# The opening of the last stage: a rewritten chain from the summed expert weights, sums moved to GpSimd, and part of a bound taken from the decoding

## The chip, the cores and the metric

One Trainium2 chip; the program runs on one of its cores. A core has TensorE (matrix products, results in the eight PSUM banks), VectorE, ScalarE and GpSimd (element by element), and SyncE, which here issues the transfers. The engines run their own instruction queues in order and wait for one another by semaphores. The metric is the device time of one execution in microseconds; before the change it is 865.24 us, the median of three runs (864.58 to 865.53).

## The reference

Eight heads of block-causal attention, then a soft mixture of experts, then a squared-ReLU feed-forward layer:

```python
scores = scale * q @ k.T;  scores = where(block_mask, scores, -1e9)
x = softmax(scores) @ v                        # (8, 8, 576, 64) -> (4608, 512)
logits = x @ phi                               # (4608, 32): 8 experts, 4 slots each
d = softmax(logits, over tokens);  slot_input = d.T @ x
slot_out[e] = relu(slot_input[e] @ w1[e]) @ w2[e]
x = softmax(logits, over slots) @ slot_out     # (4608, 512)
h = relu(x @ w_in)                             # w_in (512, 2048)
out = (h * h) @ w_out                          # w_out (2048, 512)
```

All is in float32. The slots are so few (32) that `slot_out @ w_in` can be formed first, a matrix of 32 x 2048, called `psw` in the kernel (laid out as four groups of 32 rows by 512 columns). Then `h` is the combine weights (32 wide) times that matrix.

## The kernel before, in words

Three stages follow one another: attention with the routing logits, the experts (`experts`), and the last stage (`ffn`). The change lies where the second passes into the third.

**The end of the experts.** The last weights of `w2` arrive in pieces, and `acc1` takes the products of the second group of four experts in two halves of 256 columns. Each half is copied to SBUF by ScalarE into `os` (one buffer), transposed by TensorE and copied into `so` by VectorE (`finish`), and two `fold`s per half then multiply it with `w_in` (decoded earlier, `tin`) into `psw`, one PSUM bank.

**From psw to the hidden layer.** `psw` is split into two float32r parts, `wf[0]` (rounded) and `wf[1]` (the remainder), first 128 columns, then 384; the larger piece goes through SBUF (`cts["w"]`) and GpSimd makes its two parts (lines 1408 and 1409). `spread(c)` selects one group of 32 rows for all partitions with a selector matrix `sel` (two matmuls, line 1418) and ScalarE copies it to `ws` (line 1421). `first_hidden(c)` multiplies `ws` with the combine weights of the first 512 tokens (line 1441), `relu_square` makes Relu and Square of it on ScalarE (lines 1430, 1431), and `first_product(c, a)` multiplies with the decoded `w_out` (`tt`) into the four banks of `pos` (line 1626). There are eight chunks `c` of two halves `a`.

**Decoding.** `w_out` arrives in pairs of words per number. `decode_mag` makes float32 numbers of a chunk: an Abs on ScalarE (line 234, with priority in the planner) and four operations on VectorE (lines 235, 236, 239, 242). Behind each chunk ScalarE takes the sum of absolute values of the decoded numbers (line 1397); the eight sums give a bound for the size of `w_out` (`scale_max`, line 1463), from which the power of two `beta` follows that scales the weights into float16. Through a transposition by TensorE (`scale_turn`, lines 1470 and 1482) the maximum over partitions gives `alpha` and others.

**The first four token tiles and the blocks.** The first 512 tokens are computed in float32 as above. All later tokens go in blocks of 256 through a seven-product scheme: sums and differences of four quarters of the weights (`sum_w`, T3 to T6, 128 x 2048 each), casts to a float16 high part by ScalarE (`cast_w`, B0 to B6, line 1547) and a low part by VectorE (`low_w`, L0 to L6, line 1550); and for the activations of a block, in four parts `kq`, hidden matmuls (`block_first`, H, line 1568), Relu and Square (`block_square`, q), four sums or differences of 128 x 256 (`block_sums`, s, lines 1581 and 1536), casts (`block_cast`, c, line 1591) and low parts (`block_low`, l, line 1536). Seven products (line 1604) follow for each block.

**What sets the order.** TensorE's, VectorE's and ScalarE's instructions from chunk 4 on are in the order of the string `ORDER` (its letters are those above; `h`, `g` and `m` are hidden matmuls, Relu and Square, and product of a chunk; `n`, `z`, `b`, `a` are the scale's four steps). Ahead of it, where the stage opens, and always for GpSimd, a planner puts the instructions in order by its own costs and by the place where they stand in the program; instructions with priority go first. Inside a region with a written order, instructions from outside may still fall between. The hidden matmuls, the spreads, the transposed maximum and the block's hidden matmuls share two PSUM tiles of two banks each (`bank2`); `psw`'s bank goes to whichever pool is opened first after it.

Of the kernel before, what the change touches and what calls it, by code (L numbers as in the profile page):

```python
# [23 lines left out]
def tile_attn_soft_moe_ffn(  # L24
# [31 lines left out]
    ORDER = (  # L56
# [171 lines left out]

    def decode_mag(pool, dst, raw, w):
# [5 lines left out]
        nc.vector.tensor_scalar(out=m, in0=m, scalar1=2.0 ** -15, scalar2=None, op0=ALU.max)  # L235
        nc.vector.tensor_scalar(
            out=b, in0=b, scalar1=3, scalar2=0x3FFFFFF8, op0=ALU.logical_shift_left, op1=ALU.bitwise_and
        )
        nc.vector.scalar_tensor_tensor(
            out=b, in0=hi, scalar=0xC0000000, in1=b, op0=ALU.bitwise_and, op1=ALU.bitwise_or  # L240
        )
        nc.vector.scalar_tensor_tensor(
            out=dst.bitcast(U32), in0=lo, scalar=29, in1=b, op0=ALU.logical_shift_right, op1=ALU.bitwise_or
        )

# [905 lines left out]
    def experts():  # L1151
# [117 lines left out]
        for x in acc1:  # L1269
            nc.vector.memset(x, 0.0)  # L1270
        for c in range(8):
# [92 lines left out]
    def ffn():  # L1364
# [17 lines left out]
        sums = ws_p.tile([128, KH], F32, name="sums")  # L1382
        mg = ws_p.tile([128, 2], F32, name="mg")
        sc = {nm: ws_p.tile([128, 1], F32, name=nm) for nm in ("beta", "alpha", "inv", "sg", "se")}
        sc.update(zip(("top", "sw"), cts["tiny"][2:]))
        al = [sc["alpha"]] + cts["tiny"][:2]
        wf = [d_p.tile([128, 512], F32R, name=f"wf{i}", bufs=1) for i in range(2)]
        tt = t_p.tile([128, KH, 2, DM], F32, name="t")

        def decode_wo(c, a=None):  # L1390
            sl = slice(0, 2) if a is None else slice(a, a + 1)
            w = DM * (sl.stop - sl.start)
            raw = wos[c][:, sl].rearrange("p a f x -> p (a f) x")
            decode_mag(d_p, tt[:, c, sl].rearrange("p a f -> p (a f)"), raw, w)
            if a != 0:
                jk = d_p.tile([128, 2, DM], mybir.dt.bfloat16, tag="jk", name="jk", bufs=1)
                nc.scalar.activation(out=jk, in_=tt[:, c], func=AF.Abs, accum_out=sums[:, c:c + 1])

        psw = wots["psw"]
        parts = (slice(0, 128), slice(128, 512))  # L1400
        p = parts[0]
        nc.scalar.copy(wf[0][:, p], psw[:, p])
        nc.vector.tensor_tensor(out=wf[1][:, p], in0=psw[:, p], in1=wf[0][:, p], op=ALU.subtract)
        p = parts[1]
        wfs = cts["w"][:, p]
        nc.scalar.copy(wfs, psw[:, p])
        nc.scalar.copy(cts["w"][:, parts[0]], psw[:, parts[0]])
        nc.gpsimd.tensor_copy(wf[0][:, p], wfs)
        nc.gpsimd.tensor_tensor(out=wf[1][:, p], in0=wfs, in1=wf[0][:, p], op=ALU.subtract)
        decode_wo(0, 0)  # L1410
# [4 lines left out]
        def spread(c, p=slice(0, 512)):  # L1415
            ps = bank2("ps_ws")
            for i in range(2):
                nc.tensor.matmul(
                    ps[:, p], cts["sel"][:, c, 32 * i:32 * i + 128], wf[i][:, p], start=(i == 0), stop=(i == 1)
                )  # L1420
            nc.scalar.copy(ws[:, 512 * c + p.start:512 * c + p.stop], ps[:, p])

# [9 lines left out]

        def first_hidden(c, step=1024, late=False):
            ps = bank2("ps_h")
            if late:
                hid[c] = lambda: first_square(c, ps)
            else:
                g = g_p.tile([128, 1024], F32, tag="g", name="g")
            for a in range(2):
                f = c + KH * a  # L1440
                nc.tensor.matmul(
                    ps[:, 512 * a:512 * a + T0], ws[:, 128 * f:128 * f + 128], ctt[:, 0:T0], start=True, stop=True
                )
                if step == 512:
                    relu_square(ps, g[:, 512 * a:512 * a + 512], 512 * a, 512 * a + 512, scale=1.0 / CSC)
                    if a == 0:
                        spread(2, parts[0])
            if late:
                return
            if step == 1024:  # L1450
                relu_square(ps, g, 0, 1024, scale=1.0 / CSC)
            return g

# [81 lines left out]

        sub = lambda o, a, b: nc.vector.tensor_tensor(out=o, in0=a, in1=b, op=ALU.subtract)  # L1536
# [41 lines left out]
        def block_sums(n, kq):  # L1578
            x = a7[n, kq]
            z = lambda s: x[:, :, s]  # L1580
            nc.vector.tensor_tensor(out=z(4), in0=z(1), in1=z(3), op=ALU.add)
            sub(z(1), z(0), z(1))
            sub(z(5), z(4), z(0))
            sub(z(6), z(2), z(5))

# [13 lines left out]
        def product(n, sa, sb, acc, first):  # L1599
# [9 lines left out]
        pos = [ps_o.tile([128, DM], F32, tag="o", name="po") for _ in range(N0)]  # L1609
        spread(0, parts[0])  # L1610
        hid = {0: first_hidden(0, 512)}
        decode_wo(0, 1)
        spread(0, parts[1])
        spread(2, parts[1])
        nc.vector.tensor_reduce(
            out=mg[:, 0:1], in_=wf[0].bitcast(F32), axis=AX.X, op=ALU.max, apply_absolute_value=True
        )
        spread(1)
        spread(3)
        for c in range(1, KH):  # L1620
            decode_wo(c)

        def first_product(c, a):
            g = hid[c]
            for t in range(N0):
                nc.tensor.matmul(  # L1626
# [77 lines left out]

        for c in range(3):
            hid[c + 1] = first_hidden(c + 1)
            for a in range(2):
                first_product(c, a)
        E = mybir.EngineType
# [82 lines left out]
```

## Time and profile before

| | |
|---|---|
| median of three runs | 865.24 us |
| the profiled execution | 864.24 us |
| its span | 862.4 us |
| TensorE busy | 810.9 us (94%) |
| VectorE busy | 670.2 us (78%) |
| ScalarE busy | 626.9 us (73%) |
| GpSimd busy | 241.5 us (28%) |

The profile shows one execution. In its tables PE is TensorE and PEld its weight loads, DVE is VectorE, ACT is ScalarE, POOL is GpSimd. A row of a timeline gives the start, the duration, engine, line and operation, output and input tiles with shapes, and a count; in brackets the time for which the engine stood idle before it and what ended that. Matmuls are pipelined, so the duration of one in such a row holds its way through the array, and the rate is read from several in a row. PEclk is the granted clock of TensorE as a share of 2.4 GHz. The experts end at about 464 us of the span, the last stage runs from there to the end; the string `ORDER` begins at about 496 us and the first block product stands at 536.5 us.

### The profile page before, as it was taken

The numbers are of one execution on the slowest core, as the hardware profiler recorded it, in microseconds if no ns is written. First come the engines' busy times: TensorE is split into PE (matmuls) and PEld (weight loads), VectorE is DVE, ScalarE is ACT, GpSimd is POOL, SyncE is SP. The second block draws the span as 40 slices with busy tenths as digits, with TensorE's granted clock in tenths as the row PEclk, the third lists the DMA queues.
The fourth block names the chain that finished last, engine by engine and source line by source line (L and its number), as shares of the span: only waits on it lengthen the run. The fifth ranks groups of instructions, "written<-read, shape, count | busy, mean of one in ns | idle before, by whom it ended". The sixth has DMA issues, their size and how long they took to land.

```text
span 862.4 us, 21655 instructions
## 1 busy us (share of the span) xinstructions
PE 810.9 (94%) x8741; PEld 597.5 (69%) x8741; DVE 670.2 (78%) x1546; ACT 626.9 (73%) x996; POOL 241.5 (28%) x394
## 2 busy tenths in 40 slices
PE   2699999998999999999986999999999999999997
PEld 1366767575766667676432454888888888888886
DVE  5877789899899987764726899888888888888880
ACT  5588787787878687743225899988888888878770
POOL 0255747376574757464000000000000000000000
PEclk9899999999999999999998999999999999999999
DMA  7997998989898979589899100110000000000002
GB/s 156 194 192 132 186 216 151 223 160 224 156 215 163 197 124 197 90 251 373 335 401 397 57 0 25 39 37 25 26 25 27 25 26 25 26 25 26 26 25 49
DMA packets 213316, 113.14 MB, mean 131 GB/s; under 512 B 192096, under 2 KB 194144, under 8 KB 213216
## 3 DMA queue, kind: packets, MB, share of 16 engines
q1 hardware_dynamic: 210560, 111.11, 54.0%
q8 instruction: 68, 1.11, 0.5%
q10 hardware_dynamic: 2656, 0.66, 0.4%
q14 instruction: 32, 0.26, 0.1%
HBM read 78.71 MB, written 9.44 MB: 102 GB/s over the span
## 4 chain that ended last, share of the span: by engine, by line
PE 73%; DMA 8%; ACT 6%; POOL 6%; DVE 5%; issue 2%; SPq 0%; ACTq 0%; POOLq 0%
PE ps_y L1604 15%; PE ps_z L1604 10%; PE ps_x L1604 10%; PE xm L655 8%; PE ps_sc L581 6%; DMA t<-qb 4%; PE ps_hb L1568 3%; DMA wch<-in_moe_w_dram 3%; PE sm L675 3%; POOL ul L771 3%; PE ps_max L503 2%; POOL ss L624 2%; PE po L1626 2%; PE tl L666 2%; PE ps_qT L482 2%
## 5 line engine op out<-in xcount | busy, mean ns | idle before, releaser
L1604 PEld LDWEIGHTS <-ah 128*128 128x128 f16 x1792 | 174.8, 98 | 21.9 <-issue 0.8
L619 ACT ACTIVATE p<-ps_sc,es 128x512 f32<-128x512 f32 x192 | 129.7, 685 | 59.1 <-PE ps_sc L581 29.8
L1536 DVE TENSOR_TENSOR al<-a,ah 128x1024 f16<-128x1024 f32 (+1 forms) x128 | 138.5, 1124 | 16.9 <-ACT ah L1591 15.3
L517 DVE TENSOR_REDUCE pm<-ps_max 128x4 f32<-128x512 f32 x160 | 106.0, 681 | 32.6 <-PE ps_max L511 32.3
L624 POOL TENSOR_TENSOR ss<-p 128x384 f32<-128x384 f32 (+1 forms) x128 | 85.7, 688 | 152.4 <-ACT p L619 152.0
L1591 ACT CAST ah<-a 128x1024 f16<-128x1024 f32 (+1 forms) x128 | 114.4, 936 | 15.0 <-DVE a L1536 13.4
L581 PE MATMUL ps_sc<-t,s 128*128 128x512 f16 (+3 forms) x512 | 107.0, 302 | 11.7 <-DMA t<-qb 6.6
L1697 POOL TENSOR_TENSOR ot<-u,p 128x256 f32<-128x256 f32 x16 | 12.5, 781 | 373.6 <-DVE u L1668 357.9
L1604 PE MATMUL ps_y<-bh,al 128*128 128x256 f16 x384 | 104.7, 273 | 0.0
L1604 PE MATMUL ps_y<-bh,ah 128*128 128x256 f16 x384 | 104.6, 272 | 0.0
L1604 PE MATMUL ps_y<-bl,ah 128*128 128x256 f16 x384 | 104.6, 272 | 0.0
L624 POOL TENSOR_TENSOR ss<-ss,p 128x320 f32<-128x320 f32 (+1 forms) x128 | 97.9, 765 | 16.9 <-ACT p L619 9.1
L1604 PEld LDWEIGHTS <-al 128*128 128x128 f16 x896 | 87.6, 98 | 10.2
L1430 ACT ACTIVATE r<-ps_hb,cts_h 128x1024 f32<-128x1024 f32 x64 | 71.2, 1112 | 30.0 <-PE ps_hb L1568 29.4
L655 PE MATMUL xm<-p,ar_hi 128*64 128x256 f32 (+3 forms) x512 | 87.2, 440 | 0.0
L1536 DVE TENSOR_TENSOR a<-a 128x256 f32<-128x256 f32 x192 | 76.1, 424 | 3.9
L1604 PE MATMUL ps_x<-bh,ah 128*128 128x256 f16 x256 | 69.8, 273 | 0.0
L1604 PE MATMUL ps_z<-bh,ah 128*128 128x256 f16 x256 | 69.8, 273 | 0.0
L1604 PE MATMUL ps_x<-bh,al 128*128 128x256 f16 x256 | 69.8, 273 | 0.0
L1604 PE MATMUL ps_x<-bl,ah 128*128 128x256 f16 x256 | 69.8, 273 | 0.0
L1604 PE MATMUL ps_z<-bl,ah 128*128 128x256 f16 x256 | 69.8, 273 | 0.0
L1604 PE MATMUL ps_z<-bh,al 128*128 128x256 f16 x256 | 69.8, 273 | 0.0
(275 smaller groups left out, 1779.3 us busy)
## 6 DMA issues: line engine op xcount, KB each, us to landing
wch<-in_moe_w_dram SPq DMA_DIRECT2D x18, 1024.0 KB, 10.9
ar_hi<-in_v_dram SPq DMA_DIRECT2D x64, 128.0 KB, 3.8
raw<-in_moe_w_in_dram SPq DMA_DIRECT2D x16, 512.0 KB, 5.5
out_dram<-ot SPq DMA_DIRECT2D x32, 256.0 KB, 2.1
ar_hi<-in_moe_w_dram SPq DMA_DIRECT2D x6, 1024.0 KB, 7.8
s<-s SPq DMA_DIRECT2D x32, 144.0 KB, 4.1
ar_hi<-in_k_dram SPq DMA_DIRECT2D x16, 256.0 KB, 4.5
ar_hi<-in_q_dram SPq DMA_DIRECT2D x16, 256.0 KB, 4.2
```

The lines of the kernel that those rows point to most:

```text
L517: nc.vector.tensor_reduce(out=o, in_=i, axis=AX.X, op=ALU.max)
L581: nc.tensor.matmul(ps[:, c0:c0 + w].rearrange("p (s c) -> p s c", c=128), kk[:, 2 * t + hp, :], qq[:, 2 * u0 + hp:8:2, :], start=(c0 == 0 ...
L619: exps[:] = [nc.scalar.activation(out=pt, in_=ps, func=AF.Exp, scale=es[:, 0:1])]
L624: add = lambda o, x, y: nc.gpsimd.tensor_tensor(out=o, in0=x, in1=y, op=ALU.add)
L655: nc.tensor.matmul(box["xm"][64 * hp:64 * hp + 64, 128 * t:512], vs[:, t, hp, :], r, start=(t == 0), stop=(t == 3),)
L675: nc.tensor.matmul(SM[b][32 * g:32 * g + 32, o0:o0 + w], oj, r, start=bool(start and j == 0), stop=stop, tile_position=(0, 32 * g), skip_g ...
L771: add = lambda o, x, y: nc.gpsimd.tensor_tensor(out=o, in0=x, in1=y, op=ALU.add)
L1430: nc.scalar.activation(out=r[:, c0:c1], in_=ps[:, c0:c1], func=AF.Relu, **kw)
L1536: sub = lambda o, a, b: nc.vector.tensor_tensor(out=o, in0=a, in1=b, op=ALU.subtract)
L1568: nc.tensor.matmul(ps[:, 512 * j + 256 * a:512 * j + 256 * a + 256], w[:, 128 * f:128 * f + 128], c, start=True, stop=True,)
L1591: nc.scalar.copy(v(hl[n % 2][0][:, 2 * kq:2 * kq + 2], s), v(a7[n, kq], s))
L1604: nc.tensor.matmul(acc[:, 0:HM], a[:, k], b[:, k], start=bool(first and k + j == 0), stop=(k == KH - 1 and j == 2), skip_group_check=not f ...
```

## The change

In `experts`, the transposes of the first half are done ahead of the last piece of weights, and the folds of the first half are no longer both ahead of the second half's transposes. In the last stage, the opening is written out in order for three engines (`opening`): the two-part split of the larger piece of `psw` goes to ScalarE and VectorE, spreads are done for two groups at a time with one copy, filler matmuls of 256 columns (`spin`, 7 and 5 of them) are put ahead of the first spread and the first hidden matmuls, half of the first Relu and Square goes to VectorE, and the pools of PSUM are opened in the other order. The four operations of `decode_mag` become a list to be placed. For chunks 5 to 7 the first of them also folds its maximum into `tops`, and `scale_max` makes a bound of that (three more small operations); the absolute sums by ScalarE stay for chunks 0 to 4. `sum_w` 4, 5 and 6 and the block sums of the first block go to GpSimd, and `ORDER` is changed.

```diff
     ORDER = (
-        "O h4 n m30 b g4 T3 B2 T4 z m31 B0 a B4 L2 h5 B1 H00 m40 L0 g5 L4 q00 H01 m41 L1 q01 s00 h6 "
-        "B3 H02 s01 m50 c00 T6 c01 m51 l00 g6 l01 q02 h7 L3 g7 H03 m60 s02 q03 T5 m61 c02 s03 B6 "
-        "l02 m70 c03 L6 B5 m71 l03 L5 H10 o0 o1 X P1 ...
+        "O h4 n m30 b g4 T3 B2 T4 z m31 B0 a L2 h5 B1 H00 m40 L0 g5 L1 q00 H01 m41 B3 q01 s00 h6 "
+        "L3 T5 B4 H02 s01 m50 c00 c01 m51 l00 g6 l01 L4 T6 q02 h7 g7 H03 m60 s02 q03 m61 B5 c02 s03 "
+        "L5 l02 m70 c03 B6 m71 l03 L6 H10 o0 o1 X P1 ...
...
+        kw = {} if top is None else dict(op1=ALU.max, accum_out=top)
+            lambda: nc.vector.tensor_scalar(out=m, in0=m, scalar1=2.0 ** -15, scalar2=None, op0=ALU.max, **kw),
...
+                if c == 7 and kt == 7:
+                    tail.pop(0)()
...
-            pend.append(lambda dts=dts, os_=os_: [finish(1, dts, os_)] + [fold(dt) for dt in dts])
-        pend.pop()()
+            tail.append(lambda dts=dts, os_=os_: finish(1, dts, os_))
+        for f in (lambda: fold(0), tail.pop(0), lambda: fold(1), lambda: fold(2), lambda: fold(3)):
+            f()
...
+        d0, d1 = decode_wo(0, 0), decode_wo(0, 1)
+        for f in d0:
+            f()
         psw_st.close()
+        ps_o = st.enter_context(tc.tile_pool(name="ps_o", bufs=4, space=PSUM))
         ps_h = st.enter_context(tc.tile_pool(name="ps_h", bufs=2, space=PSUM))
-        ps_o = st.enter_context(tc.tile_pool(name="ps_o", bufs=4, space=PSUM))
...
         def scale_max():
+            x, y = tops.bitcast(U32), top_b.bitcast(U32)
+            ts(out=y, in0=x, scalar1=3, scalar2=0x3FFFFFF8, op0=ALU.logical_shift_left, op1=ALU.bitwise_and)
+            nc.vector.scalar_tensor_tensor(
+                out=y, in0=x, scalar=0xC0000000, in1=y, op0=ALU.bitwise_and, op1=ALU.bitwise_or
+            )
+            ts(out=sums[:, NABS:KH], in0=top_b, scalar1=4.5, scalar2=None, op0=ALU.mult)
             nc.vector.tensor_reduce(out=sg, in_=sums, axis=AX.X, op=ALU.add)
...
-            sub(x, a, b)
+            sub(x, a, b, nc.vector if s == 3 else nc.gpsimd)
...
+            e = nc.vector if n else nc.gpsimd
+            e.tensor_tensor(out=z(4), in0=z(1), in1=z(3), op=ALU.add)
+            sub(z(1), z(0), z(1), e)
+            sub(z(5), z(4), z(0), e)
+            sub(z(6), z(2), z(5), e)
...
+        def opening():
+            p0, p1 = slice(0, 128), slice(128, 512)
+            w = cts["w"]
+            nc.scalar.copy(wf[0][:, p0], psw[:, p0])
+            dec.tensor_tensor(out=wf[1][:, p0], in0=psw[:, p0], in1=wf[0][:, p0], op=ALU.subtract)
+            nc.scalar.copy(w, psw)
+            spin(pos[0], SPINS[0])
+            spread((0, 2), p0)
+            nc.scalar.copy(wf[0][:, p1], w[:, p1])
+            for f in d1[:3]:
+                f()
+            dec.tensor_tensor(out=wf[1][:, p1], in0=w[:, p1], in1=wf[0][:, p1], op=ALU.subtract)
+            spin(pos[0], SPINS[1])
...
+            pre = spread((0, 2), p1, False)
+            pre.pop(0)()
...
+            nc.scalar.activation(out=r[:, h0], in_=ps[:, h0], func=AF.Relu, scale=1.0 / CSC)
+            dec.tensor_scalar(
+                out=r[:, h1], in0=ps[:, h1], scalar1=1.0 / CSC, scalar2=0.0, op0=ALU.mult, op1=ALU.max
+            )
+            nc.scalar.activation(out=g[:, h0], in_=r[:, h0], func=AF.Square)
+            dec.tensor_tensor(out=g[:, h1], in0=r[:, h1], in1=r[:, h1], op=ALU.mult)
+            d1[3]()
+            first_product(0, 0, (0, 1))
+            pre.pop(0)()
+            first_product(0, 0, (2, 3))
+            ds = decode_wo(1)
...
+            pre.pop(0)()
+            first_product(0, 1, (0,))
+            first_hidden(1)
+            first_product(0, 1, (1, 2, 3))
+            for f in ds:
+                f()
+            dec.tensor_reduce(
+                out=mg[:, 0:1], in_=wf[0].bitcast(F32), axis=AX.X, op=ALU.max, apply_absolute_value=True
+            )
+            spread((1, 3))
+            size(0)
+
+        with tc.manual_schedule(engines={E.PE, E.DVE, E.Activation}):
+            opening()
```

## Rows read from the trace of the kernel before

**Rows 1.** Stages: start:end, length, busy (x count) per engine, PEclk, DMA, GB/s

```profile
464.30:470.14 5.84, 1.11 (x6) 0.79 (x6) 5.58 (x8) 5.25 (x11) 1.97 (x2) 0.84 1.03 409
...
496.74:521.73 24.99, 24.20 (x72) 12.08 (x71) 24.65 (x30) 24.32 (x21) 0.00 (x0) 1.00 0.00 0
...
536.50:558.00 21.50, 21.50 (x202) 18.21 (x201) 16.95 (x32) 19.94 (x24) 0.79 (x1) 1.00 0.10 38
```

**Rows 2.** The same view in slices of 0.2 us, where the clock changes

```profile
468.20:468.40 0.20, 0.00 (x0) 0.00 (x0) 0.20 (x1) 0.20 (x1) 0.00 (x0) 0.66 0.97 389
...
475.00:475.20 0.20, 0.20 (x1) 0.12 (x1) 0.20 (x1) 0.00 (x0) 0.00 (x0) 0.78 1.23 492
```

**Rows 3.** Timeline of TensorE, 458 to 522 us

```profile
458.46 0.61 PE L1279 MATMUL po<-wch,hT 128*4 128x256 f32 x8 [0.82 <-DMA wch<-in_moe_w_dram]
...
462.31 1.92 PE L1211 MATMUL psw<-tin,so 128*32 128x512 f32 x16 [0.29 <-DVE so L1204]
...
466.20 0.44 PE L1418 MATMUL ps_ws<-wf,sel 128*128 128x128 f32 x2 [1.97 <-ACT cts_h L1407]
...
470.14 2.08 PE L1626 MATMUL po<-t,g 128*128 128x512 f32 x2 [2.06 <-ACT g L1431]
...
481.43 1.02 PE L1441 MATMUL ps_h<-cts,ws 128*128 128x512 f32 x2
...
489.61 7.03 PE L1626 MATMUL po<-t,g 128*128 128x512 f32 x16
496.07 1.02 PE L1441 MATMUL ps_h<-cts,ws 128*128 128x512 f32 x2
...
521.73 0.74 PE L1568 MATMUL ps_hb<-cts,ws 128*128 128x256 f32 x4 [0.79 <-ACT r L1430]
```

**Rows 4.** Timeline of VectorE, 460 to 522 us

```profile
460.54 0.43 DVE L235 TENSOR_SCALAR dec_mag<-dec_mag 128x512 f32<-128x512 f32 x1 [0.87 <-ACT dec_mag L234]
...
467.15 0.67 DVE L1615 TENSOR_REDUCE mg<-wf 128x1 f32<-128x512 f32 x1
467.75 1.43 DVE L239 SCALAR_TENSOR_TENSOR dec_mag<-ar_hi,dec_mag 128x1024 uint32<-128x1024 uint32 x1
...
478.47 0.69 DVE L235 TENSOR_SCALAR dec_mag<-dec_mag 128x1024 f32<-128x1024 f32 x1 [1.84 <-ACT dec_mag L234]
...
488.54 1.23 DVE L239 SCALAR_TENSOR_TENSOR dec_mag<-wo,dec_mag 128x1024 uint32<-128x1024 uint32 x1
...
495.89 0.16 DVE L1463 TENSOR_REDUCE sg<-sums 128x1 f32<-128x8 f32 x1 [1.28 <-ACT jk L1397]
...
496.66 0.16 DVE L1476 SCALAR_TENSOR_TENSOR beta<-sg 128x1 f32<-128x1 f32 x1
...
517.25 4.09 DVE L1536 TENSOR_TENSOR al<-a,ah 128x1024 f16<-128x1024 f32 x4
```

**Rows 5.** Timeline of ScalarE, 464 to 535 us

```profile
464.30 0.27 ACT L1402 CAST wf<-psw 128x128 fp32r<-128x128 f32 x1 [2.65 <-PE psw L1211]
...
497.12 1.02 ACT L1430 ACTIVATE r<-ps_h 128x1024 f32<-128x1024 f32 x1 [1.26 <-PE ps_h L1441]
...
499.14 3.88 ACT L1547 ACTIVATE bh<-t,beta 128x2048 f16<-128x2048 f32 x2
...
515.08 3.44 ACT L1591 CAST ah<-a 128x1024 f16<-128x1024 f32 x4
...
534.20 1.04 ACT L1633 COPY ot<-po 128x512 f32<-128x512 f32 x2
```

**Rows 6.** GpSimd by form: line, engine, operation, shapes, count | busy us, mean ns

```profile
L624 POOL TENSOR_TENSOR ss<-p 128x384 f32<-128x384 f32 x64 | 64.2, 1003 | 152.4 <-ACT p L619 152.0
...
L624 POOL TENSOR_TENSOR ss<-p 128x64 f32<-128x64 f32 x64 | 23.9, 373 | 0.0
...
L1409 POOL TENSOR_TENSOR wf<-cts_h,wf 128x384 fp32r<-128x384 f32 x1 | 1.3, 1332 | 0.1
```

More of the change, by code (lines that the diff above doesn't have):

```diff
@@ L234, in decode_mag @@
             nc.scalar.activation(out=m, in_=hi.bitcast(F32), func=AF.Abs)
[L235 to L244, printed above, removed]
+        kw = {} if top is None else dict(op1=ALU.max, accum_out=top)
+        return [
+            lambda: nc.vector.tensor_scalar(out=m, in0=m, scalar1=2.0 ** -15, scalar2=None, op0=ALU.max, **kw),
+            lambda: nc.vector.tensor_scalar(
+                out=b, in0=b, scalar1=3, scalar2=0x3FFFFFF8, op0=ALU.logical_shift_left, op1=ALU.bitwise_and
+            ),
+            lambda: nc.vector.scalar_tensor_tensor(
+                out=b, in0=hi, scalar=0xC0000000, in1=b, op0=ALU.bitwise_and, op1=ALU.bitwise_or
+            ),
+            lambda: nc.vector.scalar_tensor_tensor(
+                out=dst.bitcast(U32), in0=lo, scalar=29, in1=b, op0=ALU.logical_shift_right, op1=ALU.bitwise_or
+            ),
+        ]
     def setup():
@@ L1270, in experts @@
             nc.vector.memset(x, 0.0)
+        tail = []
         for c in range(8):
@@ L1383, in ffn @@
         mg = ws_p.tile([128, 2], F32, name="mg")
+        NABS = 5
+        tops, top_b = [ws_p.tile([128, KH - NABS], F32, name=nm) for nm in ("tops", "top_b")]
         sc = {nm: ws_p.tile([128, 1], F32, name=nm) for nm in ("beta", "alpha", "inv", "sg", "se")}
@@ L1393, in decode_wo @@
             raw = wos[c][:, sl].rearrange("p a f x -> p (a f) x")
[L1394 to L1397, printed above, removed]
-        psw = wots["psw"]
-        parts = (slice(0, 128), slice(128, 512))
-        p = parts[0]
-        nc.scalar.copy(wf[0][:, p], psw[:, p])
@@ L1403, in ffn @@
[L1403 to L1410, printed above, removed]
+            return decode_mag(
+                d_p, tt[:, c, sl].rearrange("p a f -> p (a f)"), raw, w, tops[:, c - NABS:c - NABS + 1] if c >= NABS else None
+            )
@@ L1415, in spread, with part @@
[L1415 to L1421, printed above, removed]
+        def spread(cs, p=slice(0, 512), run=True):
+            ps = bank2("ps_ws").rearrange("p (a f) -> p a f", a=2)
+            n = p.stop - p.start
+            o = ws.rearrange("p (c f) -> p c f", c=4)[:, cs[0]:4:2, p]
+            def part(x):
+                for i in range(2):
+                    nc.tensor.matmul(
+                        ps[:, x, 0:n], cts["sel"][:, cs[x], 32 * i:32 * i + 128], wf[i][:, p],
+                        start=(i == 0), stop=(i == 1),
+                    )
+            fs = [lambda: part(0), lambda: part(1), lambda: nc.scalar.copy(o, ps[:, :, 0:n])]
+            if not run:
+                return fs
+            for f in fs:
+                f()
@@ L1431, in relu_square, with first_hidden @@
             nc.scalar.activation(out=o, in_=r[:, c0:c1], func=AF.Square)
-        def first_hidden(c, step=1024, late=False):
+        def first_hidden(c, late=False):
             ps = bank2("ps_h")
@@ L1443, in first_hidden @@
                 )
[L1444 to L1452, printed above, removed]
+            if not late:
+                first_square(c, ps)
         def first_square(c, ps):
@@ L1534, in store @@
                     nc.sync.dma_start(out=out[r0:r0 + 64, :], in_=ot[64 * h:64 * h + 64, :])
-        sub = lambda o, a, b: nc.vector.tensor_tensor(out=o, in0=a, in1=b, op=ALU.subtract)
+        sub = lambda o, a, b, e=nc.vector: e.tensor_tensor(out=o, in0=a, in1=b, op=ALU.subtract)
         q = lambda i: tt[:, :, i // 2, HM * (i % 2):HM * (i % 2) + HM]
@@ L1609, in ffn, with first_product @@
         pos = [ps_o.tile([128, DM], F32, tag="o", name="po") for _ in range(N0)]
[L1610 to L1623, printed above, removed]
+        hid = {}
+        def first_product(c, a, ts=range(N0)):
             g = hid[c]
-            for t in range(N0):
+            for t in ts:
                 nc.tensor.matmul(
@@ L1703, in block_out @@
                 store(N0 + 2 * n + 1, ot(1))
-        for c in range(3):
-            hid[c + 1] = first_hidden(c + 1)
-            for a in range(2):
-                first_product(c, a)
+        E = mybir.EngineType
+        dec = nc.vector
+        def opening():
[11 more added lines that the diff above has]
+            spin(pos[0], SPINS[1])
+            ps = bank2("ps_h")
+            for a in range(2):
+                nc.tensor.matmul(
+                    ps[:, 512 * a:512 * a + T0], ws[:, 1024 * a:1024 * a + 128], ctt[:, 0:T0], start=True, stop=True
+                )
+            pre = spread((0, 2), p1, False)
+            pre.pop(0)()
+            r = o_p.tile([128, 1024], F32, tag="r", name="r", bufs=1)
+            g = hid[0] = g_p.tile([128, 1024], F32, tag="g", name="g")
+            h0, h1 = slice(0, 256), slice(256, 512)
+            nc.scalar.activation(out=r[:, h0], in_=ps[:, h0], func=AF.Relu, scale=1.0 / CSC)
+            dec.tensor_scalar(
+                out=r[:, h1], in0=ps[:, h1], scalar1=1.0 / CSC, scalar2=0.0, op0=ALU.mult, op1=ALU.max
+            )
+            nc.scalar.activation(out=g[:, h0], in_=r[:, h0], func=AF.Square)
[5 more added lines that the diff above has]
+            ds = decode_wo(1)
+            nc.scalar.activation(out=r[:, 512:1024], in_=ps[:, 512:1024], func=AF.Relu, scale=1.0 / CSC)
+            nc.scalar.activation(out=g[:, 512:1024], in_=r[:, 512:1024], func=AF.Square)
+            pre.pop(0)()
[3 more added lines that the diff above has]
+            for f in ds:
+                f()
+            dec.tensor_reduce(
+                out=mg[:, 0:1], in_=wf[0].bitcast(F32), axis=AX.X, op=ALU.max, apply_absolute_value=True
+            )
+            spread((1, 3))
+            size(0)
@@ L1709, in ffn @@
+        with tc.manual_schedule(engines={E.PE, E.DVE, E.Activation}):
+            opening()
+        size(1)
+        for c in range(2, KH):
+            for f in decode_wo(c):
+                f()
+            if c < NABS:
+                size(c)
+        with tc.manual_schedule(engines={E.PE}):
+            for c in range(1, 3):
+                first_hidden(c + 1)
+                for a in range(2):
+                    first_product(c, a)
         E = mybir.EngineType
```

12 lines of the change are left out of this document (5 added, 7 removed), and 2 rows, old and new, of the table ORDER.

## The prediction, made before the result was known

> **What bounds the kernel now.** I read the page's slices first, then a table of stages, then the timelines of TensorE, VectorE and ScalarE one after another, and last the forms that GpSimd runs. The profiled execution took 864.24 us for a span of 862.4, so 1.84 us lie around the span; the median of the three runs shown is 865.24, 1.0 above it. I work out differences on the profiled execution and put them on the median.
>
> From 536.5 us on TensorE is busy all the time (the last row of the stage table, 21.50 of 21.50 us [rows 1]) and nothing after that point is shortened, so the end moves by as much as the first block product moves, and that stands at 536.5. The question is which engine sets it. Between 496.74 and 521.73 TensorE is busy for 24.20 of 24.99 us, VectorE for 24.65 and ScalarE for 24.32 [rows 1]: three engines arrive together, and a change that frees one is cut off by the next.
>
> Ahead of that, TensorE is poor: of the 5.84 us after the last `psw` matmul it works 1.11 [rows 1]. It waits 1.97 us for a copy that frees `psw`'s bank and 2.06 us for the first squared activations [rows 3]. Its granted clock falls to 1.2 GHz in the slice that begins at 468.2 and is back at 2.4 GHz in the one that begins at 475.0 [rows 2], so about 6.8 us run at half speed. In full-speed work: two chunks from 481.43 to 496.07 take 14.64 us [rows 3], 7.32 each. Sixteen product passes take 7.03 with a tail, 0.43 each [rows 3]; 16 x 0.43 = 6.87 leaves 0.45 for the hidden pair, 0.22 a matmul. From the end of `psw` (462.31 + 1.92 = 464.23) to the third hidden pair at 481.43 there are 16 passes, 4 hidden matmuls and 8 spreads of 512 columns: 6.87 + 12 x 0.22 = 9.5 us of work in 17.2. So 7.7 us are lost there.
>
> **The change part by part.**
>
> *Tail of the experts.* The final quarter of the last expert matmuls starts at 458.46 after waiting 0.82 us for its weights [rows 3]. The transposes of the first half go into that wait; before, they stood behind it, and the second half's copy stood behind them. After the matmuls (459.05) come one fold, a transpose pair and three folds. Two folds take 1.92 [rows 3], so four take 3.8, and with 0.4 for the transposes `psw` ends at about 463.25: 1.0 us earlier. If VectorE's copy of the transposes falls behind a decode operation of 0.43 [rows 4], it is 0.5.
>
> *Opening on TensorE.* The first copy of 128 columns takes 0.27 [rows 5]; the copy of all of `psw` I put at 0.6. The seven warming matmuls write into the bank that `psw` held (the pools change places), so they and the spread behind them still wait for both copies; they take 0.8 (256 columns against 0.22 for 512). With 0.5 for the spread, 0.4 for its copy, 0.5 for the hidden matmul, 0.4 for Relu and 0.4 for Square of a quarter, the first product pass starts 4.0 us after `psw`, at 467.2 instead of 470.14. These are estimates scaled from the 0.27 of 128 columns and the 0.22; an error of 1 us in them changes nothing below. Warming matmuls and spreads leave no long idle, so I take the clock as staying at 2.4 GHz. Behind the first pass lie 16 passes, one hidden pair and the rest of the spreads, 8.5 us, so the third hidden pair stands at 463.25 + 4.0 + 8.5 = 475.75, 5.7 us earlier.
>
> *Where those 5.7 us go.* The next thing that TensorE needs from outside is the transposed maximum in the middle of chunk 3, and that needs `scale_max`, which VectorE can do only behind its decoding. TensorE would be there at 475.75 + 14.64 (two chunks) + 0.45 + 8 x 0.43 = 494.3. VectorE's stretch from its first decode operation (460.54) to `scale_max` (495.89) is 35.35 us [rows 4]. Out of it go the wait of 1.84 us for ScalarE and the one of 1.28 us for the last absolute sum [rows 4], and 0.3 for the two operations beside GpSimd's subtraction (one took 1.43 us against 1.23 [rows 4]). Into it come: the subtraction of 384 columns that GpSimd did, 0.5 (the reduction of 512 takes 0.67 [rows 4]); Relu and Square of 256 columns, 0.85; two waits for ScalarE's copies in the ordered opening, 0.6 and 0.65; and the folded bounds. No row shows a `tensor_scalar` that also folds. Below it lies the same operation without folding, 0.69 for 1,024 columns; above it the reduction, 0.67 for 512, so 1.3 [rows 4]. I take 1.24 (0.55 more, three times, 1.65), since a fold looks most like the reduction; the other end is nothing. Sum: 495.89 - 3.42 + 0.5 + 0.85 + 1.25 + 1.65 = 496.7. With three more small operations in `scale_max` (0.57) and the 0.93 from there to the end of the scale's own operation (496.66 + 0.16 [rows 4]), the scale is ready at 498.2. So TensorE's lead is worthless there: it waits about 3 us for VectorE.
>
> On this fold the Trainium skill (SBUF — State Buffer, Who interferes with whom) says that a `tensor_scalar` which also writes out its accumulator is not among the operations that enter the two-port mode. By that it would run at one column a cycle and cost what I took; without it the sum is 1.65 us lower. No run here shows it yet.
>
> *ScalarE behind the scale.* Before, the scale was there at 496.8, but the first cast started only at 499.14, behind chunk 4's Relu and Square, which had waited 1.26 us for TensorE [rows 5]. Now these two are done long before, and the cast starts at 498.25: 0.9 us earlier. From there ScalarE runs without a gap to the copy at 534.20 [rows 5], and its list of operations up to the last Relu that TensorE waits for (the 0.79 us at 521.73 [rows 3]) holds the same members as before. So TensorE's end of the stage moves by ScalarE's 0.9, no more. The three absolute sums that ScalarE drops lie ahead of the scale, where it has room: nothing.
>
> *Sums to GpSimd.* VectorE loses three subtractions of 2,048 columns and four sets of block sums, over 13 us, but was held by the same chain, so that gives nothing by itself. GpSimd's rows give 0.37 us for 64 columns and 1.00 for 384 [rows 6], 1.97 ns a column: 4.3 us for 2,048 columns (2.3 on VectorE), 0.75 for 256, 3.0 for a set of four. The slow end is the ratio of the 384-column subtraction beside VectorE, 1.33 to 1.00 [rows 6]: 5.7 and 4.0. In the order T4, sums 0, sums 1, T5, sums 2, T6, sums 3 only the end of the list is tight: with the first cast at 498.25, the third quarter's Square ends near 522.0, sums 2 run to 525.1, T6 to 529.4 and sums 3 to 532.5; a half cast (3.44 for four [rows 5]) and a subtraction (4.09 for four [rows 4]) behind them end at 534.5, ahead of TensorE, which is at the block product at 535.6. On the slow end each of the three steps is about 1 us longer. I take +0.2; the ends are 0 and +2.5.
>
> Sum: -0.9 + 0.2 = -0.7 us, 865.24 - 0.7 = 864.5 us.
>
> **The rivals.**
>
> *The scale comes early (faster).* If the fold costs nothing (-1.65) and the planner puts `scale_max` between the last decode operations or closes the two waits (another 0.6), the first cast starts at about 496 instead of 499.14. Then -3.1 + 0.2 = -2.9: 862.3 us. For it: ScalarE has no gap behind the cast, so all of it arrives. Against: the reduction's row.
>
> *GpSimd does T5 ahead of the second block sums (slower).* GpSimd's order is the planner's, not written out. T5 stands ahead of these sums in the list, and both are released within 0.2 us of each other: T5 by a subtraction of 2.3 us, the sums by Relu and Square of 2.2, both behind the same cast. If T5 starts after the first of the four sums, the second comes 4.3 us later. ScalarE has 3.65 us of other work there (a cast of 3.88 / 2 [rows 5] and two halves of 0.86), so against 0.75 + 4.3 + 0.75 for its next input it idles 2.2, and for the second half about 3.0 in all. The same can come at T6, 0.5. With the 0.9 gained: +2.6, 867.8 us. It decides as soon as T5's turn comes before the third of these sums. For it: the list, and VectorE's relief, which releases T5 early. Beside that stands a rule of the Trainium skill (SBUF — State Buffer, Who interferes with whom): a VectorE instruction with two SBUF inputs contends with a GpSimd instruction that reads SBUF. The pair 1.43 and 1.33 agrees with it; by it T5 would be 5.7 us and this case 1 us worse.
>
> *The clock falls while TensorE waits for the scale (slower, small).* The wait of 3 us is shorter than the sparse stretch of 4.0 us (464.2 to 468.2) after which it fell before [rows 2]. If it falls, chunk 3's second half and the next hidden pair take about 4 us more; half of that reaches ScalarE's order: +2 - 0.7 = +1.3, 866.5 us.
>
> *The change doesn't do what it says:* ScalarE's decode operations have priority, and the planner may put one ahead of a copy in the opening. It costs about 1 us there, inside the 3 us of waiting: no other time.
>
> **How the numbers follow.** Chances: my forecast 0.33, early scale 0.31, T5 first 0.28, clock 0.08. A measurement of this kernel tells 0.2%, 1.73 us, from no change. My forecast's own spread (863 to 866.5) is 0.07 faster, 0.24 same, 0.02 slower; the early scale is 0.28 and 0.03 same; T5 first is 0.04 same and 0.24 slower; the clock 0.04 and 0.04. So faster 0.35, same 0.35, slower 0.30. The range goes from 861.2 (early scale with GpSimd never late and a further 1 us) to 868.8 (T5 first on a slowed GpSimd); the likeliest case's own range is 863 to 866.5.
>
> **What would show it.** Right: `psw` ends near 463.3; the first product pass stands 4 us behind it, the granted clock 1.00 throughout; TensorE idles 2 to 4 us ahead of the transposed maximum; the first cast starts at 498.3; the folding operation takes 1.2 us; GpSimd's 2,048 columns take 4.3 us. Wrong: TensorE not waiting there; the fold at 0.7 us; a gap of over 1 us on ScalarE between the casts of the first and the second quarter; the first block product moved by more than 1.7 us either way.

## The result, and the profile after

The changed kernel takes 876.56 us, the median of 6 runs (874.27 to 879.61), against 864.91 (the median of 6, 864.09 to 866.65) for the kernel before in the same session: 1.4% slower, ratio 1.014 with a 95% interval of 1.0121 to 1.0158. The forecast was 864.5 us and the range ended at 868.8. The profiled execution took 874.27 us for a span of 872.5.

The two traces are compared from one event, the last landing of expert weights, which is the start of the last L1285 (before: L1279) group on TensorE, to the first block product. That landing moves by some us from one trace to the next (456.4 to 463.5 in those of this document): it is at 458.46 us before [rows 3] and at 456.44 after. From it the first block product stands 78.06 us off before (458.46 to 536.52) and 90.18 us after (456.44 to 546.62), 12.1 us more; the medians differ by 11.65. Behind it both traces have the same 325.9 us to their end. So the whole loss lies in this stretch. In three steps:

| from, to | before | after | difference |
|---|---|---|---|
| landing, end of `psw` | 5.77 | 4.55 | -1.22 |
| end of `psw`, first cast of weights | 34.91 | 34.76 | -0.15 |
| first cast, first block product | 37.38 | 50.87 | +13.49 |

The stages of the kernel after (columns as in [rows 1]: TensorE, its weight loads, VectorE, ScalarE, GpSimd, then the granted clock): end of `psw` to the first product; the middle stage up to the end of TensorE's longest wait, which answers roughly to 496.74:521.73 before; ten microseconds in which the clock falls; and the block products.

```profile
460.99:465.83 4.84, 3.21 (x21) 2.19 (x21) 2.74 (x7) 2.49 (x7) 0.00 (x0) 1.00 1.03 410
494.70:525.81 31.11, 20.27 (x59) 9.83 (x59) 27.59 (x24) 20.36 (x17) 22.32 (x10) 0.91 0.00 0
...
520.00:530.00 10.00, 3.18 (x8) 1.95 (x9) 6.48 (x4) 6.92 (x7) 5.57 (x5) 0.52 0.00 0
...
546.60:568.10 21.50, 21.48 (x200) 18.21 (x200) 17.83 (x32) 20.19 (x25) 0.79 (x1) 1.00 0.14 52
```

The opening went from 5.84 to 4.84 us with the granted clock at 1.00, not 0.84. In the middle stage TensorE and ScalarE, which had both filled it, now stand idle for a third of it; GpSimd works 22.32 us of it where it had done nothing. The timeline of TensorE after:

```profile
456.44 0.61 PE L1285 MATMUL po<-wch,hT 128*4 128x256 f32 x8 [0.42 <-DMA wch<-in_moe_w_dram]
...
458.21 2.78 PE L1214 MATMUL psw<-tin,so 128*32 128x512 f32 x24
...
465.83 1.98 PE L1628 MATMUL po<-t,g 128*128 128x512 f32 x4 [0.20 <-ACT g L1737]
...
495.38 0.49 PE L1482 MATMUL ps_mg<-ident,mg 128*128 128x128 f32 x2 [1.46 <-DVE mg L1477]
...
525.81 1.22 PE L1454 MATMUL ps_h<-cts,ws 128*128 128x512 f32 x2 [9.32 <-ACT r L1445]
528.04 1.22 PE L1580 MATMUL ps_hb<-cts,ws 128*128 128x256 f32 x4 [1.01 <-ACT r L1445]
529.06 16.36 PE L1628 MATMUL po<-t,g 128*128 128x512 f32 x32
...
546.62 0.27 PE L1617 MATMUL ps_x<-bh,ah 128*128 128x256 f16 x1 [0.73 <-ACT ot L1635]
```

The wait of 9.32 us for ScalarE is the main one. TensorE stood idle in it, and the granted clock from 520 to 530 us is 0.52, about the lower of its two levels (1.2 of 2.4 GHz): the 32 passes behind it take 16.36 us, where the kernel before has 13.90.

```profile
522.31 13.90 PE L1626 MATMUL po<-t,g 128*128 128x512 f32 x32
```

ScalarE itself waits for GpSimd, in its timeline after:

```profile
495.75 5.79 ACT L1559 ACTIVATE bh<-t,beta 128x2048 f16<-128x2048 f32 x3 [3.27 <-DVE beta L1488]
...
515.96 0.83 ACT L1604 CAST ah<-a 128x768 f16<-128x768 f32 x1 [3.22 <-POOL a L1548]
522.51 1.04 ACT L1604 CAST ah<-a 128x1024 f16<-128x1024 f32 x1 [5.72 <-POOL a L1548]
...
540.30 1.05 ACT L1604 CAST ah<-a 128x1024 f16<-128x1024 f32 x1 [3.27 <-POOL a L1548]
543.36 0.83 ACT L1604 CAST ah<-a 128x768 f16<-128x768 f32 x1 [2.02 <-POOL a L1548]
```

And why GpSimd is late is read from its rows and VectorE's, side by side. GpSimd after:

```profile
498.05 4.60 POOL L1548 TENSOR_TENSOR tb<-t,ta 128x2048 f32<-128x2048 f32 x1 [83.61 <-DVE ta L1548]
506.01 2.78 POOL L1594 TENSOR_TENSOR a<-a 128x256 f32<-128x256 f32 x1 [3.36 <-ACT a L1446]
508.87 7.06 POOL L1548 TENSOR_TENSOR a<-a 128x256 f32<-128x256 f32 x3
515.89 0.72 POOL L1594 TENSOR_TENSOR a<-a 128x256 f32<-128x256 f32 x1
516.57 4.51 POOL L1548 TENSOR_TENSOR ta<-t 128x2048 f32<-128x2048 f32 x1
```

VectorE after, the fold first, then the same stretch:

```profile
480.89 1.22 DVE L237 TENSOR_SCALAR_CACHE_REDUCE dec_mag<-dec_mag 128x1024 f32<-128x1024 f32 x1
482.04 0.08 DVE L237 DVE_READ_ACCUMULATOR dec_mag<-dec_mag 128x1 f32 x1
...
497.83 0.42 DVE L1494 TENSOR_REDUCE m<-ps_mg 128x2 f32<-128x256 f32 x1
498.28 4.38 DVE L1497 SCALAR_TENSOR_TENSOR se<-m 128x1 f32<-128x1 f32 x1
...
503.60 7.34 DVE L1562 SCALAR_TENSOR_TENSOR bl<-t,beta,bh 128x2048 f16<-128x2048 f32 x3
510.86 2.81 DVE L1562 SCALAR_TENSOR_TENSOR bl<-ta,beta,bh 128x2048 f16<-128x2048 f32 x1
...
516.83 5.07 DVE L1548 TENSOR_TENSOR al<-a,ah 128x768 f16<-128x768 f32 x1 [1.48 <-ACT ah L1604]
```

VectorE's operation on ONE column takes 4.38 us, and ends when GpSimd's T4 ends (498.05 + 4.60 = 502.65). GpSimd's first block sum, 0.72 us when alone (515.89), takes 2.78: the second of VectorE's three operations of 2,048 columns at 503.60 had begun 0.15 us before it (505.86), and the sum ends 0.58 us after that one (508.21). Set 0 takes 9.9 us in all (506.01 to 515.93), not 3.0. VectorE's subtraction at 516.83 takes 5.07 (0.96 alone, at 544.23) and T5 started 0.26 us before it. In these rows each of the two engines stands still for the rest of what the other has begun; that this is the cause, and not the lateness of GpSimd's results alone, is tested below.

### The profile page after: what moved, and what is told of

It reads as the page before. It is cut to its first block, busy times and chain, and to the rows that moved or that the text cites. A ratio compares the mean times of both kernels' runs of the same rounds, so it can differ in the third digit from the quotient of the medians.

```text
span 872.5 us, 21678 instructions
## 1 busy us (share of the span) xinstructions
PE 814.6 (93%) x8753; PEld 599.6 (69%) x8753; DVE 671.9 (77%) x1536; ACT 623.5 (71%) x987; POOL 276.3 (32%) x411
## 4 chain that ended last, share of the span: by engine, by line
PE 73%; POOL 9%; DVE 7%; ACT 4%; DMA 4%; issue 2%; SPq 1%; ACTq 0%; POOLq 0%
PE ps_y L1617 14%; PE ps_x L1617 10%; PE ps_z L1617 10%; PE xm L658 7%; PE ps_sc L584 6%; PE ps_hb L1580 3%; PE ps_max L506 3%; POOL ul L774 3%; PE sm L678 2%; PE ps_u L765 2%; PE ps_x L869 2%; POOL ss L627 2%; PE tl L669 2%; POOL a L1548 2%; PE ps_h L1245 2%
## 5 line engine op out<-in xcount | busy, mean ns | idle before, releaser
L1548 DVE TENSOR_TENSOR al<-a,ah 128x1024 f16<-128x1024 f32 (+1 forms) x128 | 144.9, 1172 | 21.8 <-ACT ah L1604 20.2
L1548 DVE TENSOR_TENSOR a<-a 128x256 f32<-128x256 f32 x180 | 71.4, 424 | 3.6
```

What stands on the lines that cost most here:

```text
L1548: sub = lambda o, a, b, e=nc.vector: e.tensor_tensor(out=o, in0=a, in1=b, op=ALU.subtract)
```

## The experiments

They ran in three sessions on three chips (one to four, five to eight, nine to eleven), each session with the kernel before beside them, so the ratios can be compared across sessions and the medians only within one. The cast-to-product times are first cast to first block product in their traces, one execution each (37.38 before, 50.87 after).

**One: all sums on VectorE.** The rest of the change stays, its order list too.

```diff
-            sub(x, a, b, nc.vector if s == 3 else nc.gpsimd)
+            sub(x, a, b)
-            e = nc.vector if n else nc.gpsimd
+            e = nc.vector
```

> The weights' subtractions T4 to T6 and the first block's sums go back to VectorE; everything else is the changed kernel. Both theories of the loss (GpSimd and VectorE hold each other up instruction by instruction; or GpSimd only does T5 at the wrong place) put all of it on GpSimd's share, and expect 863 to 866 us. If instead the opening or the folded bounds cost time too, it stays above 867 us. The first cast of the weights should stand where it stands in the changed kernel, and ScalarE behind it should have no gap over 1 us.

It takes 868.08 us against 866.91, ratio 1.0025 (1.0004 to 1.0045); cast to product is 41.09. So 9.78 of the 13.49 us go when GpSimd's share goes. The time is above the 863 to 866 expected, and ScalarE's trace has the place: T5, now on VectorE ahead of block sums 1 as the new list puts it, leaves ScalarE idle.

```profile
518.79 1.78 ACT L1604 CAST ah<-a 128x1024 f16<-128x1024 f32 x2 [2.32 <-DVE a L1548]
```

**Two and three: each half of GpSimd's share by itself.** Two has T4 to T6 on GpSimd and the block sums on VectorE; three is the reverse. Each takes one of the two edits above; the one shown is that of experiment three:

```diff
-            sub(x, a, b, nc.vector if s == 3 else nc.gpsimd)
+            sub(x, a, b)
```

> T4 to T6 stay on GpSimd, the block sums go back to VectorE, so nothing queues behind T5 on GpSimd. If the engines hold each other up: VectorE operations beside a T last until it ends (the first one 4.4 us for a single column, as in the changed kernel), three times up to 4.5 us on VectorE, 867 to 872 us. If only T5's place in GpSimd's queue was wrong: nothing waits behind it, at most 865 us.

> The block sums stay on GpSimd, T4 to T6 go back to VectorE. If the engines hold each other up: each of GpSimd's operations of 256 columns beside a VectorE operation of 2,048 columns takes 2.3 to 2.8 us instead of 0.7, a set of four about 9 to 10 us, and ScalarE's casts wait; 868 to 874 us. If only T5's place was wrong: a set takes 3.0 us, T5 is on another engine, at most 865 us.

Two takes 875.16 us, ratio 1.0095 (1.0065 to 1.0125), and three 875.8 us, 1.0096 (1.0061 to 1.0131). By the ratios either half costs about 0.7% over experiment one, some 6 us, so the loss is not in one kind of sum. (In the traces cast to product is 46.40 and 44.13, that is 5.3 and 3.0 over experiment one; the second trace is that of its fastest execution, 871.91 us.) In two, T4 again holds VectorE's one-column operation, and T5 a group of three block sums, now on VectorE (5.48 us, 1.22 alone):

```profile
504.74 4.39 DVE L1497 SCALAR_TENSOR_TENSOR se<-m 128x1 f32<-128x1 f32 x1
...
521.16 5.48 DVE L1548 TENSOR_TENSOR a<-a 128x256 f32<-128x256 f32 x3
```

In three, set 0 on GpSimd takes 9.26 us (510.22 to 519.48), most of it in its last three operations:

```profile
511.35 8.13 POOL L1548 TENSOR_TENSOR a<-a 128x256 f32<-128x256 f32 x3
```

**Four: GpSimd's order written out.** It is T4, sums 0, sums 1, T5, sums 2, T6, sums 3, as the prediction had assumed; T5 and T6 move in the list to match.

```diff
-        "L3 T5 B4 H02 s01 m50 c00 c01 m51 l00 g6 l01 L4 T6 q02 h7 g7 H03 m60 s02 q03 m61 B5 c02 s03 "
+        "L3 B4 H02 s01 T5 m50 c00 c01 m51 l00 g6 l01 L4 q02 h7 g7 H03 m60 s02 T6 q03 m61 B5 c02 s03 "
-        with tc.manual_schedule(engines={E.PE, E.DVE, E.Activation}):
+        with tc.manual_schedule(engines={E.PE, E.DVE, E.Activation, E.Pool}):
```

> All sums stay on GpSimd, but its order is written out too: T4, sums 0, sums 1, T5, sums 2, T6, sums 3. If only T5's place was wrong, ScalarE's wait of 5.7 us for the second set goes and TensorE's 9.3 us with it, 865 to 868 us. If the engines hold each other up, the second set merely takes its place beside VectorE's long operations, and it stays at 871 to 876 us.

It takes 880.36 us, ratio 1.0157 (1.0114 to 1.0201); cast to product is 49.28 (502.80 to 552.08). With T5 behind sums 1 the loss stays: the prediction's second rival came true in the kernel after (T5 at 516.57, behind the first sum of set 1), but it isn't the cause. ScalarE's wait of 5.72 us for set 1 is gone, and one of 5.18 stands at set 3 in its place:

```profile
527.49 4.62 POOL L1548 TENSOR_TENSOR ta<-t 128x2048 f32<-128x2048 f32 x1
```
```profile
545.76 1.04 ACT L1604 CAST ah<-a 128x1024 f16<-128x1024 f32 x1 [5.18 <-POOL a L1548]
```

**Five to seven: what the rest of the change is worth.** Five has all sums on VectorE and the order list of before; six folds besides only the last bound (NABS = 7, the edit shown), and seven none (NABS = 8, without the three operations in `scale_max`).

```diff
-        NABS = 5
+        NABS = 7
```

> All sums of the last stage on VectorE, as in e1_all_vector, and besides the order list of the kernel before; the short opening, the fold of three bounds and the tail of the experts stay as changed. Theory: what e1_all_vector lost beyond the kernel before (0.25%, some 2 us) is the changed order list alone (the alpha chain behind T4, T5 ahead of block sums 01, which left ScalarE idle for 2.32 us at 518.79), while opening, fold and tail give the 1.4 us by which the first cast came nearer to the last landing (39.3 us against 40.7). Then this is 0.5 to 2.5 us under the kernel before: ratio 0.997 to 0.9995, and H10 starts 75 to 77 us behind the last landing of weights (77.2 before, 79.5 in e1_all_vector). Rival: the fold and the opening cost what e1_all_vector lost, whatever the order: ratio 1.001 to 1.004 again, H10 at 79 or later.

> As e5_vector_old_order, but only the last chunk's bound is folded from VectorE's first decode operation; the sizes of chunks 5 and 6 are ScalarE's abs sums again. Theory: VectorE's decode is what the scale waits for, so two folds fewer (0.53 us each, 1.22 against 0.69) bring the scale 1.0 us sooner behind the last landing, and the time 0.5 to 1 us under e5. Rival: ScalarE, with two abs sums more (1.08 and 0.22 us each), is late for its decode or hidden work instead, and the time is the same as e5 within 0.5 us, or up to 1.5 us more.

> As e5_vector_old_order, but nothing is folded: the sizes of all eight chunks are ScalarE's abs sums, as in the kernel before, and scale_max has three operations fewer. Theory: the fold costs VectorE 1.6 us in three operations and 0.5 us in scale_max, and saves the last abs sum between VectorE's last decode operation and the scale (some 1.5 us with its semaphores), so it is worth about nothing: this is e5 within 0.7 us. Rival: the fold is what brings the first cast forward, and this is 1 us or more above e5.

The medians are 865.38, 864.5 and 865.35 against 867.1; the ratios are 0.998 (0.9962 to 0.9999), 0.9967 (0.9946 to 0.9988) and 0.9977 (0.9959 to 0.9994). The first shows that, with the sums on VectorE, the new list costs 2.95 us (41.09 to 38.14 from cast to product). Of the 0.76 us that are left over the kernel before, 0.63 match a wait that it does not have: the first cast now comes as soon as the scale is there, and behind the casts that need no T4 ScalarE waits 0.63 us for it. Experiment eleven takes this wait out. From the end of `psw` to the first cast the three traces have 34.74, 33.71 and 34.25 us, before 34.91: two folds cost 1.03, as expected, and the shortest is the one that folds only the last. The medians alone can't tell the three apart.

**Eight: GpSimd's work without its results.** All real sums are on VectorE as in five, and GpSimd does 16 subtractions of 256 columns that nobody reads.

```diff
             e = nc.vector
+            if n == 0:
+                for i in range(4):
+                    sub(spare, z(2), z(3), nc.gpsimd)
```

> As e5_vector_old_order, all real sums on VectorE, but with each of the four block sums of the first block GpSimd does four subtractions of 128x256 (f16 out) into a scratch tile that nobody reads: 16 operations, some 0.72 us each when alone, 11.5 us in all. Nobody waits for them. Theory (GpSimd and VectorE hold each other up for whole instructions): VectorE's operations beside them start or end late by about GpSimd's busy time, and the time is 4 to 11 us above e5. Rival (GpSimd alone is held up, and the loss came from ScalarE waiting for its late results): VectorE's durations are as in e5, and so is the time, within 1 us.

It takes 871.68 us, ratio 1.0046 (1.0022 to 1.0069): 6.3 us above five by the medians; cast to product is 43.22, 5.1 more. Nobody waits for GpSimd here, so the rival, that the loss came only from waiting for its late results, falls. Four neighbouring groups of VectorE in five, without GpSimd:

```profile
526.03 2.34 DVE L1562 SCALAR_TENSOR_TENSOR bl<-ta,beta,bh 128x2048 f16<-128x2048 f32 x1
528.29 0.41 DVE L1594 TENSOR_TENSOR a<-a 128x256 f32<-128x256 f32 x1
528.74 1.22 DVE L1548 TENSOR_TENSOR a<-a 128x256 f32<-128x256 f32 x3
529.87 2.28 DVE L1548 TENSOR_TENSOR ta<-t 128x2048 f32<-128x2048 f32 x1
```

The same four in eight:

```profile
529.62 2.81 DVE L1562 SCALAR_TENSOR_TENSOR bl<-ta,beta,bh 128x2048 f16<-128x2048 f32 x1
532.35 0.95 DVE L1597 TENSOR_TENSOR a<-a 128x256 f32<-128x256 f32 x1
533.34 2.58 DVE L1548 TENSOR_TENSOR a<-a 128x256 f32<-128x256 f32 x3
535.84 2.81 DVE L1548 TENSOR_TENSOR ta<-t 128x2048 f32<-128x2048 f32 x1
```

Each VectorE operation, whatever its length, is 0.4 to 0.5 us longer: two sums of 256 columns take turns, one by one. VectorE loses 7.6 us so (2.58 - 1.22 and its like, ten groups). Of TensorE's 5.1 us, 1.0 is in the 32 passes (14.90 us against 13.89, behind two waits for ScalarE of 1.88 and 1.51), so some 4 of the 7.6 arrived as waiting; I estimate that VectorE had 2.5 to 3.5 us to spare.

**Nine and ten: which operations hold each other.** Nine is eight with copies in place of the subtractions; ten is five with 16 spare subtractions while VectorE decodes.

```diff
-                    sub(spare, z(2), z(3), nc.gpsimd)
+                    nc.gpsimd.tensor_copy(spare, z(2))
```
```diff
             opening()
+        spare = cts["ws"][:, 0:256]
+        for i in range(16):
+            sub(spare, cts["w"][:, 0:256], cts["w"][:, 256:512], nc.gpsimd)
```

> As e8_spare_gpsimd, but GpSimd's 16 spare operations are copies (one input, 128x256, f16 out) instead of subtractions (two inputs); nobody reads them. Theory (the hold is between operations that read two tensors): VectorE's forms stay as in e5 (0.42, 2.29, 2.34 us) and the time is within 1 us of e5's ratio 0.998. Rival (any GpSimd operation on SBUF holds VectorE): each VectorE operation beside one grows as in e8, by about 0.5 us, and the time is again 4 to 7 us above e5.

> As e5_vector_old_order, but GpSimd does 16 spare subtractions of 128x256 (f16 out, two inputs, nobody reads them) behind the opening, while VectorE decodes: two operations with one input (0.69, with the fold 1.21 us) and two with two inputs (1.22 us) per 1,024 columns. Theory: the operations with two inputs grow to about 1.75 us beside them, those with one input stay at 0.69. Rival: all four forms grow by 0.5. Either way VectorE sets the scale, so the scale and the end come later by what VectorE loses: 3 to 8 us by the theory, 6 to 11 by the rival.

Nine takes 864.09 us against 865.47, ratio 0.9988 (0.9973 to 1.0004); cast to product is 38.34. The time is five's, as the theory had it, but the durations are not: the forms do grow, by 0.08 to 0.20 us an operation, 2.3 us in all.

```profile
526.06 0.61 DVE L1597 TENSOR_TENSOR a<-a 128x256 f32<-128x256 f32 x1
526.71 1.57 DVE L1548 TENSOR_TENSOR a<-a 128x256 f32<-128x256 f32 x3
```

Ten takes 869.25 us against 865.47, ratio 1.0052 (1.003 to 1.0074). My theory of two inputs falls: the one-input `tensor_scalar` goes from 0.69 to 1.22 and the two-input operation from 1.22 to 1.75, both by 0.53. The reduction beside them stays at 0.68 (0.67 before [rows 4]), and at 485.07, once GpSimd is done (464.81 + 19.26 = 484.07), 0.68 is back.

```profile
469.84 1.22 DVE L237 TENSOR_SCALAR dec_mag<-dec_mag 128x1024 f32<-128x1024 f32 x1
...
473.25 1.75 DVE L241 SCALAR_TENSOR_TENSOR dec_mag<-ar_hi,dec_mag 128x1024 uint32<-128x1024 uint32 x1
...
477.73 0.68 DVE L1752 TENSOR_REDUCE mg<-wf 128x1 f32<-128x512 f32 x1
...
485.07 0.68 DVE L237 TENSOR_SCALAR dec_mag<-dec_mag 128x1024 f32<-128x1024 f32 x1
```

The first cast stands 44.62 us behind the landing, 5.3 more than in five, and the product 82.75 against 77.43, the same 5.3.

**Eleven: a better version.** It is six with the alpha chain ahead of T4, and with the cast and low part of quarter 1 ahead of those of T4.

```diff
-T3 B2 T4 z m31 B0 a B4 L2 h5 B1 H00 m40 L0 g5 L4 q00 H01 m41 L1 q01
+T3 B2 z m31 B0 a T4 L2 h5 B1 H00 m40 L0 g5 B4 L1 q00 H01 m41 L4 q01
```

> As e6_fold_last_only (all sums on VectorE, the order list of before, only the last bound folded), with the alpha chain moved ahead of T4 on VectorE and the casts and lows of the second quarter (1) ahead of those of T4: in e6 and e5 ScalarE waited 0.63 us for T4 and TensorE 0.87 us for the alpha chain's first reduction. Theory: ScalarE's list sets the end of the stage, so its 0.63 us arrives: 0.5 to 0.7 us under e6, ratio 0.9955 to 0.9965. Rival: another wait takes its place (T4's cast is needed no later than before by the lows), and it is e6 within 0.3 us.

It takes 862.25 us against 865.47, ratio 0.997 (0.9954 to 0.9987): faster than both kernels, like six. In the trace cast to product is 37.25, 0.89 less than in six: ScalarE's wait of 0.63 is gone, and TensorE's 0.87 gave way to one of 0.67 for ScalarE. Whether that arrives in the time, these intervals can't tell; the ratio is no lower than six's.

## Why the prediction was wrong

**The step that failed** is "*Sums to GpSimd* … I take +0.2; the ends are 0 and +2.5". In place of +0.2, experiment one shows 9.78 us between the first cast and the first block product. GpSimd's durations alone were right: 0.72 and 4.5 to 4.6 us where 0.75 and 4.3 stood. What failed is what happens beside VectorE. The sum had a price for GpSimd's lateness and no term at all for what VectorE loses, only its relief of over 13 us. I took [rows 6]'s 1.33 against 1.00 us and [rows 4]'s 1.43 against 1.23 as a rate, GpSimd a third slower beside VectorE. They were remainders of whole operations. This is the pair in the kernel before, GpSimd first, then VectorE:

```profile
466.76 1.33 POOL L1409 TENSOR_TENSOR wf<-cts_h,wf 128x384 fp32r<-128x384 f32 x1
```
```profile
466.36 0.87 DVE L236 TENSOR_SCALAR dec_mag<-dec_mag 128x1024 uint32<-128x1024 uint32 x1
467.15 0.67 DVE L1615 TENSOR_REDUCE mg<-wf 128x1 f32<-128x512 f32 x1
467.75 1.43 DVE L239 SCALAR_TENSOR_TENSOR dec_mag<-ar_hi,dec_mag 128x1024 uint32<-128x1024 uint32 x1
```

GpSimd's subtraction starts while L236 (itself held by an earlier cast) has 0.47 us to go and gets 0.33 longer; the reduction passes untouched; L239 starts 0.34 before GpSimd is done (468.09) and gets 0.20 longer. In both pairs the later operation grows by the overlap less 0.14 us. T4 in the kernel after fits the same count: VectorE's one-column operation starts 4.37 us before T4 is done (502.65) and grows by 4.38 - 0.16 = 4.22, the overlap less 0.15. A rate of a third could not make 4.38 out of 0.16. In the new stage the two engines overlap all along. Experiment eight gives the price of a subtraction of 256 columns: VectorE arrives behind its start and is held for about 0.52 us, 2.03 ns a column; T4's 4.22 is 2.06 ns a column. VectorE does the same sums in 0.42 and 2.28 us itself. So, in this kernel, moving a sum away costs VectorE more than doing it, wherever VectorE is busy with an operation that is held.

The rule was at hand, and I used half of it. The Trainium skill (SBUF — State Buffer, SBUF: two separate sides) says that of a GpSimd instruction that reads SBUF and a VectorE instruction that has two inputs there or runs in a two-port mode, whichever starts first has the shared pair of ports for the whole instruction and the other blocks fully. I quoted that the two contend and then priced it as slowing, "1 us worse". The runs agree with it in each part that they touch: 4.38 us for one column, `tensor_scalar` held (0.69 to 1.22 us), `tensor_reduce` not (0.68). The Trainium skill (SBUF — State Buffer, Who interferes with whom) also has it that the folding form does not enter a two-port mode; that it is free beside GpSimd no run here shows.

**The second rival** (T5 ahead of the second block sums) happened, and its own price was +2.6 us. Experiment four took it out, and cast to product fell by 1.6 of 13.5, while the ratio did not fall (1.0157 against 1.014); it could not have made the result. A gap of over 1 us on ScalarE between the casts of the first two quarters, one of the prediction's signs of being wrong, is there (5.72), but it says only that ScalarE waits, not why.

**The clock rival** came as a consequence: not in the wait for the scale (1.46 us, not 3) but behind the 9.32 us, where 32 passes took 2.5 us more than before (16.36 against 13.90).

**The order list** is a second term that stood at nothing. I held that ScalarE's list "holds the same members as before" and so costs nothing. Experiments one and five show 2.95 us for the new list with the sums on VectorE. What it costs in the kernel after, where GpSimd has the sums, stays open: the old list with the sums on GpSimd was not run.

**What held.** From the landing, `psw` ends 1.22 us earlier (1.0 predicted); the first pass stands 4.8 us behind it at clock 1.00 (4.0 predicted); the fold takes 1.22 (1.24), and TensorE waits for VectorE ahead of the transposed maximum, though 1.46 us where 2 to 4 stood. The scale is ready 0.9 us later than before, counted from the landing (1.4 predicted), and the first cast follows it at once, as the prediction had it. Landing to first cast is 1.37 us shorter where 0.9 was predicted; all but 0.15 of it is the experts' tail, since opening and three folds nearly cancel: without folds (experiment seven) the way from `psw` to the cast is 0.66 shorter than before, and the folds take 0.49 of that back.

## What to carry to other kernels

By these runs, work moved from VectorE to GpSimd is off VectorE's path only while VectorE is idle or reducing; beside two-input operations and plain `tensor_scalar` in SBUF, price each moved sum at nearly GpSimd's whole duration on VectorE too, and GpSimd at the rest of what VectorE has begun. Before a ratio is taken from two slowed rows, lay their starts and ends beside each other: a small excess may be the remainder of a full stop. When an operation of one column takes microseconds, look at the other engine's row that ends with it.

## What the runs showed of the hardware

A VectorE reduction from SBUF ran at 0.68 us beside GpSimd's subtractions, as alone; one from PSUM ran at 0.42, but the overlap was only 0.2 us (497.83 against T4 at 498.05). A GpSimd copy of 256 columns (float32 to float16) held VectorE for 0.08 to 0.20 us in experiment nine, against about 0.52 for a subtraction; the 16 copies took 2.3 us from VectorE, which fitted into what it had to spare, and cost no time that could be measured. A `tensor_scalar` with an accumulator takes 1.22 us for 1,024 columns where the plain one takes 0.69.
